# Gate chain with operands in PSUM, whole GpSimd pieces, a later transposition, and a new order of loads and mixes in step 0

## The chip, the core and the metric

One core of one Trainium2 chip. The metric is device microseconds of one launch, as the median of several runs; less is better. The core's engines work side by side, each through its own list of instructions in order: TensorE (PE, matmuls, results in PSUM), VectorE (DVE), ScalarE (ACT), GpSimd (POOL), and SyncE (SP), which here only issues DMAs. [...]

## What is computed

```python
def _attn_ref(x, w_r, w_i, b_r, b_i):              # x: 8 x 2496 x 256
    X = np.fft.rfft(x, axis=1)
    Yr = Xr @ w_r - Xi @ w_i + b_r
    Yi = Xr @ w_i + Xi @ w_r + b_i
    Yr, Yi = (np.sign(v) * np.maximum(np.abs(v) - 0.01, 0) for v in (Yr, Yi))
    return np.fft.irfft(Yr + 1j * Yi, n=2496, axis=1)

def _moe_ref(x, w_gate, w1, w2, capacity):         # x: 19968 x 256, 8 experts, F = 1024
    logits = x @ w_gate
    expert_idx = np.argmax(logits, axis=1)
    gate_w = softmax(logits)[np.arange(N), expert_idx]
    out = np.zeros((N, D))
    for e in range(E):                             # capacity = 80
        tok_idx = the 80 tokens of expert e with the largest gate_w
        out[tok_idx] = gate_w * (relu(x[tok_idx] @ w1[e]) @ w2[e])
    return out
```

A Fourier mix of each of 8 batches, then a mixture of experts of which only 8 x 80 tokens give a row of the output; the other rows are zero.

## The kernel before, in words

The transform of length 2496 = 39 x 64 is done as matmuls. **A** (`stageA`, `stageAz`) does the 39-point part of a batch in 6 calls on loads `xt` (`loadX`, three loads of three DMAs to a batch, two calls of A to each). ACT and DVE split its result into two f16 halves (tile `zs`), which SP stores to the DRAM buffer `zd`. `loadZ` reads `zd` back in another layout (tile `z`). **B** (`stageB`, four calls) does the 64-point part into tile `XT`. **C** (`stageC`, four calls: two halves `eh` of the columns, real and imaginary `ri`) multiplies by the weights, with the soft threshold in the eviction by ACT (`tp`) and DVE (`R`); POOL then makes the sums that `stageTs` forms and tile `YT`. **D** (`stageD`) multiplies by the identity beside the gate's weights, which gives `YO` and the gate's part `Gs`. **HB** (`stageHB`) is the last transform of `YO`, stored to the DRAM tables `hd`.

The gate's logits go through their own small inverse transform, the **gate chain** of a batch: `stageE1a` (sum), `stageE1b` (matmuls, and a trip through DRAM `gd`), `stageE2` (logits, softmax and the choice of the expert, on DVE and ACT) and `stageE3` (a transposition into `sall`). For the last batch `stageG0`, `stageG1` and `stageE1c` replace the first two. `level1` and `level2` pick the largest gates of each expert from `sall`, and the chosen tokens are gathered from `hd` and go through the experts.

A step is one half of a batch's classes: `steps` has 16, (batch, ch). In step i, C of step i stands in the code together with B of step i + 1, D of step i - 1, HB, and A of a later batch (`doC`, `doB`, `doD`, `doHB`, `doA`). A scheduler in the compiler orders each engine's list from that code and its own estimate of times; DMAs given to `pin` keep the order of the code. `psum()` hands out one of four PSUM tiles of 128 x 1024 f32. `zfill` issues the writes of zeros to the output, 56 in all, four in each of steps 1 to 14. `prepW` splits each expert's weights into halves: ACT makes the upper one, POOL (line 788) subtracts it to give the lower one. The output's writes of the chosen rows come last.

The lines that matter: L272 loads of x, L303 stores to `zd`, L314 and L316 loads of `z`, L328 to L330 matmuls of B, L282 of A, L384 of C, L398 C's eviction on DVE, L709 to L719 `stageE2` on DVE, L725 and L728 `stageE3`, L568 and L509 HB, L477 D of the last step, L855 the first instruction of `level1`.

Of the kernel before, what the change touches and what calls it, by code (L numbers as in the profile page):

```python
# [132 lines left out]
def fourier_mix_then_moe(ctx, tc, x, w_r, w_i, b_r, b_i, wg, w1, w2, t1, t2, vq, v3, v0, v1f, vt, sg, cst, cb, out):  # L133
# [133 lines left out]
    def loadX(b, c, xt=None):  # L267
        if xt is None:
            xt = zaq.tile([117, 8, 256], F32, name="xt", bufs=3)
        xv = x[b].rearrange("(a n) d -> a n d", n=64)  # L270
        for s, n in spans(c):
            pin(nc.sync.dma_start(xt[39 * s:39 * s + 39, :n], xv[:, 22 * s + 8 * c:22 * s + 8 * c + n]))  # L272
        return xt
# [11 lines left out]
    zx = []  # L285

    def stageAz(b, q, K, ng, pt):
        if b == 0 and q in (3, 4, 5):
            if q == (3, 4, 5)[0] or (q == 5 and True):
                zx.append(wkb.tile([128, 2, 11, 256], F16, name="YO", bufs=2).rearrange("p h j e -> p (h j e)"))  # L290
            i = (3, 4, 5).index(q) % 2
            zs = zx[-1][:117, 2048 * i:2048 * i + 2048].rearrange("p (g h d) -> p g h d", g=4, h=2)
        else:
            zs = zaq.tile([117, 4, 2, 256], F16, name="zs", bufs=3)
        pv = pt.rearrange("p (g d) -> p g d", d=256)
        nc.scalar.activation(zs[:K, :ng, 0, :], pv[:K, :ng], AF.Copy)  # L296
        nc.vector.tensor_tensor(zs[:K, :ng, 1, :], pv[:K, :ng], zs[:K, :ng, 0, :], op=ALU.subtract)  # L297
        flush()

        def store():  # L300
            for s in range(K // 39):
                n0 = 22 * s + 4 * q
                nc.sync.dma_start(zd[b][:, n0:n0 + ng], zs[39 * s:39 * s + 39, :ng].rearrange("p g h d -> p g (h d)"))  # L303
        stores.append(store)
# [279 lines left out]
    def stageE1a(b, Gs):  # L584
        G = ek.tile([128, 20, 8], F32, name="G", bufs=1)
        nc.vector.tensor_reduce(out=G, in_=Gs.rearrange("p c q (h e) -> p c e (q h)", e=8), op=ALU.add, axis=AX.X)
        gp = ek.tile([128, 2, 20, 8], F16, name="gp", bufs=2)
        nc.scalar.activation(gp[:, 0], G, AF.Copy)
        nc.vector.tensor_tensor(gp[:, 1], G, gp[:, 0], op=ALU.subtract)
        return gp  # L590
# [5 lines left out]
    def stageG0(b, YT):  # L596
# [8 lines left out]
        G = ek.tile([128, 20, 8], F32, name="gex")[:, :11]  # L605
# [6 lines left out]
    def stageG1(b, R, eh):  # L612
# [10 lines left out]
        else:  # L623
            u7 = u7s[0]
            nc.vector.tensor_tensor(u7, pv, u7, op=ALU.add)
# [9 lines left out]
    def stageE1b(b, gp):  # L635
# [7 lines left out]
        gu = ek.tile([128, 2, 48], F32, name="gdif")  # L643
# [4 lines left out]
        nc.scalar.activation(gu, pt[:, 48:144].rearrange("p (t f) -> p t f", t=2), AF.Copy, scale=sc)  # L648
        nc.scalar.activation(gh[:64, 18:21], pt[:64, 512:536].rearrange("p (a e) -> p a e", a=3), AF.Copy, scale=sc)
        nc.vector.scalar_tensor_tensor(gu[:, 1], gu[:, 1], -1.5, at(0), op0=ALU.mult, op1=ALU.add)  # L650
        for a, f in ((1, g), (2, -g)):
            nc.vector.scalar_tensor_tensor(at(a), gu[:, 0], f, gu[:, 1], op0=ALU.mult, op1=ALU.add)
# [42 lines left out]
    def stageE2(b, gr, last=False):  # L695
# [16 lines left out]
        nc.vector.tensor_reduce(out=q, in_=ex, op=ALU.add, axis=AX.X)  # L712
        nc.vector.scalar_tensor_tensor(q, q, 1e-9, unit[:78, 0:1].to_broadcast([78, 32]), op0=ALU.add, op1=ALU.mult)
        nc.vector.reciprocal(q, q)
        rk = rank[:78].unsqueeze(1).to_broadcast([78, 32, 8])
        nc.vector.scalar_tensor_tensor(d, d, 0.0, rk, op0=ALU.is_ge, op1=ALU.mult)
        nc.vector.tensor_reduce(out=m, in_=d, op=ALU.max, axis=AX.X)
        nc.vector.tensor_tensor(d, d, bc(m), op=ALU.is_equal)
        twos.append(nc.vector.tensor_tensor(sc.rearrange("p e n -> p n e"), d, bc(q), op=ALU.mult))  # L719
# [22 lines left out]
    def prepW(e, pool, name):  # L742
# [20 lines left out]
        def step(k, i):  # L763
# [549 lines left out]
    xls.append((Xq[0], loadX(*Xq.pop(0))))  # L1313
# [5 lines left out]
    hold.clear()  # L1319
    preX()  # L1320
# [6 lines left out]
    for i in range(len(steps)):  # L1327
# [26 lines left out]
        def doC(eh, ri, s=None):  # L1354
# [5 lines left out]
            if ri == 1 and b < B - 1:  # L1360
                stageTs(ch, RR[eh], YT, eh)
# [75 lines left out]
        if i == 0:  # L1437
            znext = loadZ(*steps[2])
            hold.clear()
        if i <= 1:  # L1440
            doA(1)
# [4 lines left out]
        if i:  # L1446
            znext = loadZ(*steps[i + 2]) if i + 2 < len(steps) else None
# [46 lines left out]
    stageE3(p[0], sc6)  # L1494
# [6 lines left out]
    with tc.high_priority():  # L1501
        stageE3(b, sc)
# [90 lines left out]
```

## Time and profile before

| | |
|---|---|
| median of 3 runs | 640.14 us (637.53 to 642.4) |
| profiled execution | 635.39 us, of which the span of the instructions is 633.6 us |
| PE busy | 546.1 us, 86% |
| DVE busy | 406.7 us, 64% |
| ACT, POOL busy | 302.7 us, 315.2 us |
| moved by DMA | 133.12 MB, mean 210 GB/s |
| mean granted TensorE clock | 0.931 |

A share of the span is a mean over stages of different kinds: 0 to 100 us the first batches come in, 100 to 500 us the steps run, and then the last gate chain, the choice of tokens and the experts follow each other. So the stages are read one by one.

### The profile page before, as it was taken

The numbers are of one execution on the slowest core, as the hardware profiler recorded it, in microseconds if no ns is written. First come the engines' busy times: TensorE is split into PE (matmuls) and PEld (weight loads), VectorE is DVE, ScalarE is ACT, GpSimd is POOL, SyncE is SP. The second block draws the span as 40 slices with busy tenths as digits, with TensorE's granted clock in tenths as the row PEclk, the third lists the DMA queues.
The fourth block names the chain that finished last, engine by engine and source line by source line (L and its number), as shares of the span: only waits on it lengthen the run. The fifth ranks groups of instructions, "written<-read, shape, count | busy, mean of one in ns | idle before, by whom it ended". The sixth has DMA issues, their size and how long they took to land. (4 is left out here: it accounts for less than half of the span.)

```text
span 633.6 us, 12704 instructions
## 1 busy us (share of the span) xinstructions
PE 546.1 (86%) x4925; PEld 383.8 (61%) x4926; DVE 406.7 (64%) x748; ACT 302.7 (48%) x442; POOL 315.2 (50%) x310
## 2 busy tenths in 40 slices
PE   7366959999999999999999989987899984968791
PEld 2144527676766776686767657765677772526681
DVE  3432525466667667578656996875998847866860
ACT  2322525554545464554446544545566753601560
POOL 2000444444445453544445344575974697647681
PEclk8786978999999999999999999998999975969997
DMA  7796779689679968987997789699754584628830
GB/s 170 268 210 159 205 201 285 196 227 253 200 219 273 267 182 192 304 254 187 249 243 228 199 213 268 169 257 263 238 151 116 150 273 155 204 54 293 297 107 31
DMA packets 95912, 133.12 MB, mean 210 GB/s; under 512 B 26494, under 2 KB 77717, under 8 KB 93973
## 3 DMA queue, kind: packets, MB, share of 16 engines
q1 hardware_dynamic: 88341, 114.59, 67.2%
q10 hardware_dynamic: 5376, 8.39, 4.6%
q0 software_dynamic: 2128, 9.25, 4.3%
q8 instruction: 41, 0.67, 0.4%
q14 instruction: 26, 0.21, 0.1%
HBM read 69.57 MB, written 62.63 MB: 209 GB/s over the span
## 5 line engine op out<-in xcount | busy, mean ns | idle before, releaser
L384 PE MATMUL ps<-XT,WM 128*128 128x288 f16 (+1 forms) x1536 | 217.0, 298 | 8.0 <-DVE R L398 4.7
L384 PEld LDWEIGHTS <-WM 128*128 128x128 f16 x1536 | 149.2, 98 | 66.6 <-issue 12.8
L401 POOL TENSOR_TENSOR R<-R,sgs 128x576 f32<-128x576 f32 x28 | 35.8, 1280 | 183.5 <-DVE R L398 183.4
L398 DVE SCALAR_TENSOR_TENSOR R<-ps,thr,tp 128x674 f32<-128x674 f32 (+1 forms) x56 | 48.4, 864 | 96.1 <-ACT tp L392 94.0
L424 POOL TENSOR_TENSOR YT<-R,YT 128x1408 f16<-128x1408 f32 (+1 forms) x28 | 73.5, 2624 | 36.3 <-ACT YT L423 36.3
L392 ACT ACTIVATE tp<-ps,thr 128x674 f32<-128x674 f32 (+1 forms) x64 | 49.7, 777 | 87.5 <-PE ps L384 87.2
L282 PE MATMUL ps<-xt,t1f 117*117 117x512 f32 (+1 forms) x170 | 86.2, 634 | 3.9 <-DMA xt<-in_x 3.9
L328 PE MATMUL ps<-t2s,z 128*128 128x128 f16 (+1 forms) x320 | 60.3, 225 | 28.8 <-DMA z<-zd 21.1
L297 DVE TENSOR_TENSOR zs<-ps,zs 117x1024 f16<-117x1024 f32 (+1 forms) x45 | 51.0, 1135 | 27.2 <-ACT zs L296 26.1
L334 DVE TENSOR_TENSOR XT<-ps,XT 128x640 f16<-128x640 f32 (+2 forms) x64 | 51.9, 814 | 15.1 <-ACT XT L333 15.1
L296 ACT ACTIVATE zs<-ps 117x1024 f16<-117x1024 f32 (+1 forms) x45 | 43.0, 957 | 38.8 <-PE ps L282 34.7
L333 ACT ACTIVATE XT<-ps 128x640 f16<-128x640 f32 (+2 forms) x64 | 44.9, 702 | 33.9 <-PE ps L330 22.7
L329 PE MATMUL ps<-t2s,z 128*128 128x128 f16 (+1 forms) x320 | 60.2, 225 | 0.0
L330 PE MATMUL ps<-t2s,z 128*128 128x128 f16 (+1 forms) x320 | 60.1, 225 | 0.0
L328 PEld LDWEIGHTS <-z 128*128 128x128 f16 (+1 forms) x320 | 32.1, 100 | 37.5 <-DMA z<-zd 21.2
L423 ACT ACTIVATE YT<-R 128x1408 f16<-128x1408 f32 (+1 forms) x28 | 35.5, 1268 | 36.2 <-POOL R L420 35.9
L534 PE MATMUL ps<-YO,vqs 128*128 128x512 f16 (+1 forms) x252 | 49.5, 338 | 3.3 <-DVE R L398 3.3
L492 DVE TENSOR_TENSOR YO<-ps,YO 128x768 f16<-128x768 f32 (+1 forms) x50 | 45.3, 906 | 5.2 <-ACT YO L491 5.2
L282 PEld LDWEIGHTS ps<-xt,t1f 117*117 117x117 f32 (+1 forms) x170 | 29.2, 188 | 31.4 <-issue 30.3
L481 PE MATMUL ps<-wgi,YT 128*128 128x136 f16 (+1 forms) x302 | 42.8, 225 | 1.0 <-POOL YT L424 1.0
L534 PEld LDWEIGHTS <-vqs 128*128 128x128 f16 x252 | 24.9, 101 | 30.6 <-issue 14.4
L480 PE MATMUL ps<-wgi,YT 128*128 128x144 f16 (+1 forms) x302 | 43.2, 229 | 0.0
(274 smaller groups left out, 939.9 us busy)
## 6 DMA issues: line engine op xcount, KB each, us to landing
out<-zero SPq DMA_DIRECT2D x48, 384.0 KB
hd<-hs SPq DMA_DIRECT2D x94, 192.0 KB
zd<-zs SPq DMA_DIRECT2D x114, 156.0 KB
xt<-in_x SPq DMA_DIRECT2D x48, 312.0 KB
z<-zd SPq DMA_DIRECT2D x16, 576.0 KB
wt<-in_moe_w ACTq DMA_DIRECT2D x10, 512.0 KB
z<-zd SPq DMA_DIRECT2D x7, 704.0 KB
z<-zd SPq DMA_DIRECT2D x7, 640.0 KB
```

The costliest lines, as they stand in the source:

```text
L282: nc.tensor.matmul(pt[:K, 512 * j:512 * j + 512], t1f[:K, :K], xv[:, 2 * j:2 * j + 2], start=True, stop=True)
L297: nc.vector.tensor_tensor(zs[:K, :ng, 1, :], pv[:K, :ng], zs[:K, :ng, 0, :], op=ALU.subtract)
L328: nc.tensor.matmul(o, zz(0), t2s[:K, cl, 0, :], start=True, stop=False)
L329: nc.tensor.matmul(o, zz(0), t2s[:K, cl, 1, :], start=False, stop=False)
L330: nc.tensor.matmul(o, zz(1), t2s[:K, cl, 0, :], start=False, stop=True)
L334: nc.vector.tensor_tensor(ov(1), pv, ov(0), op=ALU.subtract)
L384: nc.tensor.matmul(pt[:, 512 * k:512 * k + n], WM[:, dh, m, wh, 128 * eh:128 * eh + 128], XT[:, dh, xh, c, c0 + n * k:c0 + n * k + n], sta ...
L392: nc.scalar.activation(fv(t), pv, AF.Relu, bias=thr[:, eh, ri, 0:1])
L398: nc.vector.scalar_tensor_tensor(fv(Rf), pv, thr[:, eh, ri, 1:2], fv(t), op0=ALU.add, op1=ALU.min)
L424: nc.gpsimd.tensor_tensor(yv(1), rv, yv(0), op=ALU.subtract)
L492: dvs.append(nc.vector.tensor_tensor(yol, yy, yoh, op=ALU.subtract))
L534: nc.tensor.matmul(o, tab[:, v], yo(h), start=(i == 0), stop=(i == 2))
```

## The change

Three groups of edits. In step 0 and ahead of it: the first load of x is cut in two along the order in which A uses it; all three loads of batch 1 are issued before step 0, those of batch 2 only after `loadZ` of batch 1 (list `hold`); step 0 is written out on its own, with A of batch 1 between its C, then B of step 1, `loadZ`, and the last C; step 1 gets two more A; the writes of zeros start in step 3, and steps 3 to 10 have five each. In the gate chain: the intermediate tiles that DVE reads and writes lie in PSUM (`G`, `u7`, `best`, `place`, `qs`), `stageE1b` reads PSUM without the copy to `gu`, and `stageE2` finds the expert before it needs the exponentials. And `prepW` gives POOL whole pieces of 1024 columns instead of four of 256 for experts 2 to 7, and `stageE3` of batch 6 stands behind D and HB of the last step, next to that of batch 7.

```diff
@@ loadX
-        for s, n in spans(c):
-            pin(nc.sync.dma_start(xt[39 * s:39 * s + 39, :n], xv[:, 22 * s + 8 * c:22 * s + 8 * c + n]))
+        cuts = (0, 4, 8) if (b, c) == (0, 0) else (0, 8)
+        for lo, hi in zip(cuts, cuts[1:]):
+            for s, n in spans(c):
+                pin(nc.sync.dma_start(xt[39 * s:39 * s + 39, lo:min(hi, n)], xv[:, 22 * s + 8 * c + lo:22 * s + 8 * c + min(hi, n)]))
@@ stageE1a
-        G = ek.tile([128, 20, 8], F32, name="G", bufs=1)
+        G = psum()[:, :160].rearrange("p (c e) -> p c e", e=8)
@@ stageG0
-        G = ek.tile([128, 20, 8], F32, name="gex")[:, :11]
+        G = pt[:, 512:600].rearrange("p (c e) -> p c e", e=8)
@@ stageG1
-            u7 = u7s[0]
-            nc.vector.tensor_tensor(u7, pv, u7, op=ALU.add)
+            u7 = pt[:, 512:632].rearrange("p (t f) -> p t f", t=5)
+            nc.vector.tensor_tensor(u7, pv, u7s[0], op=ALU.add)
@@ stageE1b
-        nc.scalar.activation(gu, pt[:, 48:144].rearrange("p (t f) -> p t f", t=2), AF.Copy, scale=sc)
...
-        nc.vector.scalar_tensor_tensor(gu[:, 1], gu[:, 1], -1.5, at(0), op0=ALU.mult, op1=ALU.add)
+        nc.vector.scalar_tensor_tensor(gu, pt[:, 96:144], -1.5 * sc, at(0), op0=ALU.mult, op1=ALU.add)
         for a, f in ((1, g), (2, -g)):
-            nc.vector.scalar_tensor_tensor(at(a), gu[:, 0], f, gu[:, 1], op0=ALU.mult, op1=ALU.add)
+            nc.vector.scalar_tensor_tensor(at(a), pt[:, 48:96], f * sc, gu, op0=ALU.mult, op1=ALU.add)
@@ stageE2
-        nc.vector.tensor_reduce(out=q, in_=ex, op=ALU.add, axis=AX.X)
-        nc.vector.scalar_tensor_tensor(q, q, 1e-9, unit[:78, 0:1].to_broadcast([78, 32]), op0=ALU.add, op1=ALU.mult)
+        best, place, = (pt[:78, 256 * k:256 * k + 256].rearrange("p (n e) -> p n e", e=8) for k in (1, 2))
+        qs = pt[:78, 768:800]
+        rk = rank[:78].unsqueeze(1).to_broadcast([78, 32, 8])
+        nc.vector.tensor_tensor(best, L, bc(m), op=ALU.is_ge)
+        nc.vector.tensor_tensor(place, best, rk, op=ALU.mult)
+        nc.vector.tensor_reduce(out=m, in_=place, op=ALU.max, axis=AX.X)
+        nc.vector.tensor_tensor(best, place, bc(m), op=ALU.is_equal)
+        nc.vector.tensor_reduce(out=qs, in_=ex, op=ALU.add, axis=AX.X)
+        nc.vector.tensor_scalar(q, qs, 1e-9, None, op0=ALU.add)
         nc.vector.reciprocal(q, q)
-        rk = rank[:78].unsqueeze(1).to_broadcast([78, 32, 8])
-        nc.vector.scalar_tensor_tensor(d, d, 0.0, rk, op0=ALU.is_ge, op1=ALU.mult)
-        nc.vector.tensor_reduce(out=m, in_=d, op=ALU.max, axis=AX.X)
-        nc.vector.tensor_tensor(d, d, bc(m), op=ALU.is_equal)
-        twos.append(nc.vector.tensor_tensor(sc.rearrange("p e n -> p n e"), d, bc(q), op=ALU.mult))
+        twos.append(nc.vector.tensor_tensor(sc.rearrange("p e n -> p n e"), best, bc(q), op=ALU.mult))
@@ prepW
-                m = 256 if e >= 2 else 1024
-                for j in range(0, 1024, m):
-                    nc.gpsimd.tensor_tensor(wl[:, k, c + j:c + j + m], wt[:, j:j + m], wh[:, k, c + j:c + j + m], op=ALU.subtract)
+                nc.gpsimd.tensor_tensor(wl[:, k, c:c + 1024], wt, wh[:, k, c:c + 1024], op=ALU.subtract)
@@ ahead of the steps
-    xls.append((Xq[0], loadX(*Xq.pop(0))))
+    for _ in range(2):
+        xls.append((Xq[0], loadX(*Xq.pop(0))))
...
     znext = loadZ(*steps[1])
-    hold.clear()
-    preX()
+    xls.append((Xq[0], loadX(*Xq.pop(0))))
+    hold.append(1)
@@ step 0, instead of the mix of the other steps
+            doC(0, 0); doA(2)
             consts2()
+            doC(0, 1, None, False); doA(2)
+            doC(1, 0); doA(2)
+            flush()
+            with tc.issue_after(evs[-1].ins):
+                stageTs(ch, RR[0], YT, 0)
+            for _ in Bl:
+                doB()
+            znext = loadZ(*steps[2])
+            hold.clear()
+            preX()
+            doC(1, 1)
+            prev = (b, ch, YT)
+            XT = XTn
+            continue
@@ the first of the four places of zfill() in a step; the other three have the first edit alone
-        if i > 0:
+        if i > 2:
+            zfill()
+        if 3 <= i <= 10:
             zfill()
@@ behind the steps
-    stageE3(p[0], sc6)
     doHB()
...
     with tc.high_priority():
+        stageE3(p[0], sc6)
         stageE3(b, sc)
```

**SP, step 0, what stands ahead of the load of `z` for batch 1.** `zd_85` is batch 1's buffer, `xt` a load of x, `z_650` and `z_602` the tile of step 2. Before, behind the first three stores of batch 1:

```order
L272 DMA xt<-in_x 39x1536 x2
L272 DMA xt<-in_x 39x1024
L303 DMA zd_85<-zs 39x2048 x6
L272 DMA xt<-in_x 39x2048 x3
L303 DMA zd_85<-zs 39x2048 x6
L272 DMA xt<-in_x 39x2048 x3
L303 DMA zd_85<-zs 39x1024 x2
L314 DMA z_650<-zd_85 64x11x512
```

and now, from the last constant on:

```order
L237 DMA cbs<-in_cb 128x10
L306 DMA zd_85<-zs 39x2048 x12
L306 DMA zd_85<-zs 39x1024 x2
L317 DMA z_602<-zd_85 64x11x512
L319 DMA z_602<-zd_85 64x10x512
L274 DMA xt<-in_x 39x2048 x6
L317 DMA z_994<-zd_85 64x9x512
```

The two loads of batch 2 (the rows 39x2048 x3) stood ahead of the load of `z` and stand behind it now; no load of x lies between batch 1's stores any more.

**DVE, step 0.** Each row ends one piece of PE's work, and PE's list has the pieces in nearly the same order: `XT` is B, `zs` is A, `R` is C. Before, from the end of step 0's own B on:

```order
L334 TENSOR_TENSOR XT<-ps,XT 128x2x320 x2
L398 SCALAR_TENSOR_TENSOR R<-ps,thr,tp_132 128x674
L334 TENSOR_TENSOR XT<-ps,XT 128x2x320
L297 TENSOR_TENSOR zs<-ps,zs 117x4x256
L334 TENSOR_TENSOR XT<-ps,XT 128x2x320
L398 SCALAR_TENSOR_TENSOR R<-ps,thr,tp_133 128x674
```

and now:

```order
L300 TENSOR_TENSOR zs<-ps,zs 117x4x256 x2
L401 SCALAR_TENSOR_TENSOR R<-ps,thr,tp_132 128x674
L401 SCALAR_TENSOR_TENSOR R<-ps,thr,tp_133 128x674
L300 TENSOR_TENSOR zs<-ps,zs 117x4x256 x2
L401 SCALAR_TENSOR_TENSOR R<-ps,thr,tp_132 128x674
L300 TENSOR_TENSOR zs<-ps,zs 117x4x256
L300 TENSOR_TENSOR zs<-ps,zs 78x2x256
L337 TENSOR_TENSOR XT<-ps,XT 128x2x320 x2
L337 TENSOR_TENSOR XT<-ps,XT 128x2x256 x2
L401 SCALAR_TENSOR_TENSOR R<-ps,thr,tp_133 128x674
L401 SCALAR_TENSOR_TENSOR R<-ps,thr,tp_132 128x576
```

All six A of batch 1 stand ahead of the first B of step 1, which was the second piece; the last row, step 1's first C, stands ahead of step 2's B.

**PE, the last gate chain.** `hs` is the last batch's transformed gate, the rows with `gr` and `Gs` behind it are `stageE3` of batches 7 and 6. Before:

```order
L699 MATMUL ps<-hs_6211,v1fs 78x256
L699 MATMUL ps<-hs_6211,v1h 78x256
L725 MATMUL ps<-ident,Gs 128x78 x2
L568 MATMUL ps<-YO,v3s 128x512
L568 MATMUL ps<-YO,v3s 128x256
L477 MATMUL ps<-ident,R 128x128 x18
```

and now, where the 24 rows of L512 that follow here are not shown:

```order
L701 MATMUL ps<-hs_6189,v1fs 78x256
L701 MATMUL ps<-hs_6189,v1h 78x256
L571 MATMUL ps<-YO,v3s 128x512
L571 MATMUL ps<-YO,v3s 128x256
L480 MATMUL ps<-ident,R 128x128 x18
```

```order
L731 MATMUL ps<-ident,Gs 128x78 x2
L731 MATMUL ps<-ident,gr 128x78 x2
L571 MATMUL ps<-YO,v3s 128x512
L571 MATMUL ps<-YO,v3s 128x256
```

HB and D follow the last batch's logits at once; both transpositions, of batch 6 and of batch 7, stand behind them.

## Rows read from the trace of the kernel before

**Rows 1.** Stages: busy us of each engine, granted clock, DMA share, GB/s.

```profile
44.50:52.30 7.80, 0.00 (x0) 0.00 (x1) 0.92 (x1) 0.82 (x1) 0.00 (x0) 0.70 1.00 186
...
52.33:57.82 5.49, 5.49 (x24) 3.18 (x25) 0.82 (x1) 0.90 (x2) 0.00 (x0) 0.50 0.75 182
...
92.59:98.78 6.19, 6.19 (x17) 2.61 (x18) 0.86 (x1) 1.02 (x1) 0.00 (x0) 0.50 0.95 227
...
126.00:153.00 27.00, 27.00 (x223) 18.74 (x222) 16.33 (x22) 13.58 (x17) 11.66 (x10) 1.00 0.95 248
```

**Rows 2.** PE in steps 0 and 1, in order of time; in brackets idle time and what ended it.

```profile
52.33 0.27 PE L328 MATMUL ps<-t2s,z 128*128 128x128 f16 x1 [7.87 <-DMA z<-zd]
...
58.38 0.22 PE L330 MATMUL ps<-t2s,z 128*128 128x128 f16 x1
58.43 3.64 PE L384 MATMUL ps<-XT,WM 128*128 128x337 f16 x24
...
78.69 3.66 PE L282 MATMUL ps<-xt,t1f 117*117 117x512 f32 x8 [0.50 <-DMA xt<-in_x]
...
92.59 0.29 PE L328 MATMUL ps<-t2s,z 64*128 64x128 f16 x1 [7.29 <-DMA zd<-zs]
```

**Rows 3.** SP's issues of DMAs, 28 to 101 us, in order of time.

```profile
30.97 1.40 SPq L272 DMA_DIRECT2D xt<-in_x  x3
...
79.58 0.72 SPq L303 DMA_DIRECT2D zd<-zs  x2
86.09 0.59 SPq L314 DMA_DIRECT2D z<-zd  x1
```

**Rows 4.** The page's DMA issues: count and size of one.

```profile
out<-zero SPq DMA_DIRECT2D x48, 384.0 KB
...
xt<-in_x SPq DMA_DIRECT2D x48, 312.0 KB
```

**Rows 5.** DVE, two rows of the last step, then the last gate chain, in order.

```profile
505.43 0.76 DVE L407 TENSOR_TENSOR R<-tp,XT 128x576 f32<-128x576 f32 x1 [1.45 <-ACT XT L403]
...
506.29 1.04 DVE L409 TENSOR_TENSOR R<-R,sgs 128x576 f32<-128x576 f32 x1
...
519.77 0.41 DVE L710 TENSOR_TENSOR gdif<-ps,gm 78x256 f32<-78x256 f32 x1
...
524.42 6.38 DVE L716 SCALAR_TENSOR_TENSOR gdif<-gdif,rank 78x256 f32<-78x256 f32 x1
...
534.13 0.41 DVE L716 SCALAR_TENSOR_TENSOR gdif<-gdif,rank 78x256 f32<-78x256 f32 x1
...
541.54 0.87 DVE L855 MAX8 cv<-sall 128x8 f32<-128x312 f32 x2
```

**Rows 6.** POOL's subtractions by shape: busy us, mean ns of one.

```profile
L788 POOL TENSOR_TENSOR pair<-wt,pair 128x1024 bf16<-128x1024 f32 x8 | 17.2, 2144 | 5.0 <-ACT pair L780 5.0
L788 POOL TENSOR_TENSOR pair<-wt,pair 128x256 bf16<-128x256 f32 x20 | 13.1, 683 | 0.0
```

**Rows 7.** POOL at the end of the steps, first and last of seven such rows.

```profile
504.21 3.65 POOL L788 TENSOR_TENSOR pair<-pair,pair 128x256 bf16<-128x256 f32 x4 [4.07 <-ACT pair L780]
...
525.46 5.04 POOL L788 TENSOR_TENSOR pair<-pair,pair 128x256 bf16<-128x256 f32 x8
```

**Rows 8.** PE in the last gate chain, in order of time.

```profile
522.64 1.05 PE L699 MATMUL ps<-hs,v1h 39*78 39x256 f32 x2
532.85 0.52 PE L725 MATMUL ps<-ident,Gs 78*128 78x78 f32 x2 [9.16 <-DVE Gs L719]
533.17 2.85 PE L568 MATMUL ps<-YO,v3s 128*128 128x512 f32 x4
...
540.80 0.35 PE L725 MATMUL ps<-ident,gr 78*128 78x78 f32 x2
```

**Rows 9.** DVE's groups of instructions, 120 to 500 us: busy us, mean ns of one, idle before.

```profile
L719 DVE TENSOR_TENSOR gr<-gdif,gq 78x256 f32<-78x256 f32 x6 | 14.5, 2411 | 0.2
```

**Rows 10.** The longest of PE's waits, 120 to 500 us: us in total, times, longest.

```profile
PE ps L384 <- DVE R L398: 4.7, 3, 2.4
```

More of the change, by code (lines that the diff above doesn't have):

```diff
@@ L285, in fourier_mix_then_moe @@
     zx = []
+    evs = []
     def stageAz(b, q, K, ng, pt):
@@ L295, in stageAz @@
         pv = pt.rearrange("p (g d) -> p g d", d=256)
-        nc.scalar.activation(zs[:K, :ng, 0, :], pv[:K, :ng], AF.Copy)
+        evs.append(nc.scalar.activation(zs[:K, :ng, 0, :], pv[:K, :ng], AF.Copy))
         nc.vector.tensor_tensor(zs[:K, :ng, 1, :], pv[:K, :ng], zs[:K, :ng, 0, :], op=ALU.subtract)
@@ L642, in stageE1b @@
         gh = ek.tile([128, 21, 8], F32, name="gh", bufs=1)
-        gu = ek.tile([128, 2, 48], F32, name="gdif")
+        gu = ek.tile([128, 48], F32, name="gdif")
         sc = 2.0 / S / XS
@@ L1352, in fourier_mix_then_moe, with doC @@
         RR = {}
-        def doC(eh, ri, s=None):
+        def doC(eh, ri, s=None, sums=True):
             if ri == 0:
@@ L1360, in doC @@
             if ri == 1 and b < B - 1:
-                stageTs(ch, RR[eh], YT, eh)
+                if sums:
+                    stageTs(ch, RR[eh], YT, eh)
             elif ri == 1 and not end:
@@ L1406, in fourier_mix_then_moe @@
         pend = [(p[0], stageE1b(*p)) for p in pend]
-        if i > 0:
+        if i > 2:
             zfill()
         doC(0, 1); doD(); doHB(); doB(); doD()
-        if i == 0:
-            doA(3)
         doP(); doW({12: 1, 13: 1, 14: 1}.get(i, 1))
-        if i > 0:
+        if i > 2:
             zfill()
@@ L1419, in fourier_mix_then_moe @@
         sc = None
-        if i > 0:
+        if i > 2:
             zfill()
-        if i == 0:
-            doA(1)
         doC(1, 1)
-        if i == 0:
-            hold.append(1)
         doA(); doHB()
-        if i == 0:
-            flush()
         if pend and not end:
@@ L1436, in fourier_mix_then_moe @@
             pend3 = [(p[0], sc)]
[L1437 to L1441, printed above, removed]
+        if i == 1:
+            doA(2)
         if prev and pch == 1:
@@ L1445, in fourier_mix_then_moe @@
             doHB()
-        if i:
-            znext = loadZ(*steps[i + 2]) if i + 2 < len(steps) else None
+        znext = loadZ(*steps[i + 2]) if i + 2 < len(steps) else None
         if p1 is None and not (Aq or Xq or xls):
```

## Prediction

> **What bounds the kernel now.** The page comes first: PE is busy for 86% of 633.6 us, so about 88 us are PE's waits and its lower clock, and the question is where they lie. The table of stages and PE's list in time put the first ones ahead of 100 us. PE stands still for 7.87 us ahead of 52.33 and for 7.29 us ahead of 92.59, each time until a tile `z` is there [rows 2]. In the first of these stretches PE did nothing while the DMA engines' share was 1.00 at 186 GB/s [rows 1]: data, not PE, set the pace. [...] With the 0.50 us for a load of x [rows 2] the two places cost 7.87 + 7.29 + 0.50 of idle time and half of 5.49 and of 6.19 in slow work: 21.5 us in all.
>
> The list of SP's DMAs tells why `z` is late. For the first it stands behind a load of x of batch 1, issued at 30.97; for the second it was issued at 86.09, 6.5 us after the last stores of `zd` at 79.58 that it needs; PE could start another 6.5 us later, at 92.59 [rows 2, 3]. The stores came late because A of batch 1 was spread over step 0, its last calls at 78.69 [rows 2].
>
> From 100 to 500 us PE works without a gap to speak of: 27.00 of 27 us in the stretch from 126 us, with the DMA engines at 0.95 of their time there [rows 1]. An edit there pays only through PE's waits, of which the longest group is 4.7 us in 380 [rows 10].
>
> The second place is the last gate chain. PE has the last batch's logits at 523.69 (522.64 + 1.05) and then waits 9.16 us, for `Gs` [rows 8]. DVE's list shows what it does meanwhile: one instruction, L716 of batch 6, takes 6.38 us, and the same instruction of batch 7 at 534.13 takes 0.41 [rows 5]. POOL subtracts weights without a gap from 504.21 to 530.50 (525.46 + 5.04) [rows 7], and L716 ends 0.3 us after that. It has two inputs in SBUF; L710, with one input in PSUM, took 0.41 in the midst of POOL's work [rows 5]. So I read it as DVE locked out by POOL. Behind the wait come `stageE3` of batch 6, HB and D of the last step, and only at 540.80 `stageE3` of batch 7 [rows 8]; `level1` starts at 541.54 [rows 5]. From there to the end runs one chain of DVE, DMA and experts, which the change shifts but for POOL's weights.
>
> [...]
>
> **The change, part by part.**
>
> *Step 0.* All six A of batch 1 now stand ahead of the first B of step 1. The first load of x of batch 1 is issued where it was, at about 31 us; with 312 KB each [rows 4], three DMAs take 5.0 us at 186 GB/s, and the second three stand behind them. I let A start at 42.5 and put the rest by PE's prices. Six A at 1.83 (half of 3.66) less the short last one, 10 us; two C of step 0 that are left and stand among them, 7.3; that gives the last A at about 63 with some 3 us for loads. B of step 1 has 54 matmuls, 0.055 us apart (58.38 to 58.43), 3 us; C(1,1) and step 1's first C 3.64 each [rows 2]: PE comes to the B of step 2 at 72.8. The last stores are issued a little over a us after A's end and need the 6.5 us of before to land (79.58 to 86.09 [rows 3]), so they are there at 71 to 73; the load of `z` then takes the 6.5 us of before, and B can start at 77 to 81. I take 79.5. PE is idle for 6.7, has half of some 6.2 us at the lower clock (3.1), and finds the load of batch 2's x, now behind `z`, about 2.8 late (0.94 MB at 227 GB/s [rows 1], 4.1 us, with little of B to do meanwhile). With 0.4 for small waits that is 13.0 against 21.5: **−8.5**. If `z` comes at 76 and the clock stays up, about 8 are left of the 21.5 (−13); if it comes at 87, 14.2 + 3.1 + 2.8 + 0.4 (−1).
>
> *The first load cut in two* saves at most what A's first call waits for, while its third still needs the whole; SP issues three more DMAs. 0, ±1, in the range.
>
> *Zero writes.* Steps 1 and 2 lose eight, steps 3 to 10 gain one each, 384 KB [rows 4], 1.55 us of all DMA engines at 248 GB/s. The stretch of 27 us at 0.95 and 248 GB/s [rows 1] has 1.35 us free; the mean of the span is 210 GB/s, so others have more. **+1**, from 0 (hidden) to +4 (0.2 us too much in some steps, and `z` late).
>
> *Gate chain of batches 0 to 5.* L719 takes 2.41 us there [rows 9] against 0.41 of L710 [rows 5]; it now has a PSUM operand. The chain loses some 2 us of DVE per batch, and PE waited for DVE's `R` 4.7 us in all [rows 10]. One more DVE instruction per chain costs 0.4, and the PSUM slot is held for some 4 us, with three others free. **−2**, from 0 to −4.
>
> *Whole pieces on POOL.* A piece of 1024 takes 2.14 us, one of 256 takes 0.68 [rows 6]: POOL's sum falls (four are 2.7), but an instruction of DVE with two SBUF inputs that meets one may wait up to 2.14. In the last step L409 at 506.29 took 1.04 where L407 ahead of it, of the same size, took 0.76 [rows 5], on the path to the last gate. Three or four such instructions stand there: **+1.5**, 0 to +5. `level1` has them too: **+1**, 0 to +3. The experts' last pieces end later: **+0.5**, 0 to +1.5.
>
> [...]
>
> *The last gate chain.* L716 and its followers get an operand in PSUM, so the price is that of L710, 0.41, and the chain of batch 7, whose rows stood behind those of batch 6, can begin at 523.7. Ten instructions of about 0.4 with one trip to ACT end it at about 529. PE in the meantime does HB and D, which took 7.6 us from 533.17 to 540.80 [rows 8]: from 523.7 to 531.3. Now PE is what ends last; both `stageE3` follow at once (0.52 + 0.35), then one copy more than the 0.4 us between 541.15 and `level1`, which starts at 533.3 in place of 541.54: **−8**. If POOL still holds half of L716's wait the chain ends at 532 and −7 is left; if whole pieces stop DVE's few instructions left with two SBUF operands, −4; at best, if HB and D go quicker with no wait ahead of them, −11.
>
> [...]
>
> **The sum.** −8.5 + 1 − 2 + 1.5 + 1 + 0.5 − 8 = −14.5. The profiled execution took 635.4 us, so it would take 620.9; the median stands 4.7 above it, and I put the same difference on it: 640.1 − 14.5 = **625.6**.
>
> **Rivals.** *The start stays bound by the DMA engines* (0.14): the same bytes pass before `z`, at a share of 1.00 [rows 1]; what moves is their order, and two loads of x come earlier. Then `z` of step 2 is not there before 87, the first part is −1 to −3, and with the rest −6: about 632. For it: the first wait had nothing but DMA in it; against: the second is put down to a store's landing [rows 2], and that store moves. *The best case* (0.12): `z` at 76 and full clock, −13, and −10 in the tail: 616. *Whole pieces lock DVE out* (0.08): each of some ten instructions with two SBUF inputs in the last step and `level1` waits 1.5 us longer (2.14 − 0.68 [rows 6]), +15 in place of the +2.5 above: 640.1 − 14.5 + 12.5, about 638. It decides once such waits fall on the path at every meeting. *PSUM operands don't free DVE* (0.02): the edit doesn't do what it says, L716's wait remains, and `stageE3` moved back can't help; middle and tail bring nothing: 640.1 − 8.5 + 1 = 633. *The denser zero writes* (0.05), the slower side: once the DMA engines' share in a step of 28 us passes 1 (1.55 us more at 0.95 is 1.007), the load of `z` falls behind from step to step; a wait of 1.6 us may then be followed by some 5 us lost in slow work besides (5.49 and 6.19 us at 0.50 cost 3 each [rows 1], twice that at the most). In four steps that is 26 us: 651. Against it: the next stretches have more room, and the loads of `z` are issued a step ahead.
>
> **How the numbers follow.** The forecast has 0.59. Its own terms reach from 613 (−13, −10, −4) to 632; the rivals at 632 and 633 lie inside a range of **613 to 637**, which leaves out the slower side (0.05), most of the rival at 638 (0.08) and some 0.05 of spread between runs (637.5 to 642.4 before). About 1% is what a measurement of this kernel can tell from no change: faster means below 633.7. Forecast and best case are (0.71), and of the two near 632 and 633 (0.16) somewhat over half, 0.09: faster 0.80; the rest of them and the rival at 638 make same 0.15; slower 0.05.
>
> **What would show it.** Right: the first B of step 2 starts near 79.5, with one long wait of PE ahead of it, and the wait at 52 is gone; L716's successors take about 0.4 while POOL works; PE goes from the last logits into HB without a gap, and the first row of `level1` starts some 16 us earlier than 541.5 (8.5 from the start, 8 from the tail, less the middle). Wrong: `z` of step 2 past 85; DVE instructions of 2 us and more at 505 to 515 or in `level1`; waits of PE for `z` in steps 3 to 10; POOL's work lasting longer into the gate chain.

## The result, and the profile after

The changed kernel took 635.75 us (median of 20 runs, 629.3 to 640.64), the kernel before 640.85 (20 runs): ratio 0.9899, 95% interval 0.9873 to 0.9924, or 6.5 us less (4.9 to 8.1) where 14.5 were forecast. The ratio leaves out runs in a slower state, so it is not that of the medians, and the profiled execution of the changed kernel is such a run: 640.64 us with a span of 638.9, the longest of its 20. Each reading of it below is therefore set beside the profiles of the experiments; of those, e3's is 4 us above the median of its runs and e8's 6 us below.

The start. PE's list in time, as in [rows 2]: start, us, line, operation, and in brackets idle time and what ended it.

```profile
47.54 1.95 PE L284 MATMUL ps<-xt,t1f 117*117 117x512 f32 x4 [3.03 <-DMA xt<-in_x]
...
83.82 0.23 PE L331 MATMUL ps<-t2s,z 64*128 64x128 f16 x1
...
85.47 0.23 PE L331 MATMUL ps<-t2s,z 128*128 128x128 f16 x1 [1.31 <-DMA z<-zd]
...
92.93 3.73 PE L284 MATMUL ps<-xt,t1f 117*117 117x512 f32 x4 [6.45 <-DMA xt<-in_x]
```

The wait of 7.87 us is gone; 3.03 us for x stand in its place, ahead of the first A of batch 1. B of step 2, which started at 92.59, starts at 83.82 and has the rest of its `z` at 85.47. But the A between the first two B of step 2 waits for x until 92.93, which is where PE stood before, and its four matmuls then take 3.73 us at a granted clock of 0.50 (eight took 3.66 in the kernel before [rows 2], where the clock was 1.00 from 78.69 to 82.35). The two stretches by stage, as in [rows 1], with the granted clock as a share of TensorE's full speed, and SP's issues ahead of them, as in [rows 3]:

```profile
80.79:93.00 12.21, 4.45 (x45) 3.35 (x42) 2.69 (x3) 3.67 (x4) 7.06 (x5) 0.75 1.10 176
92.93:97.00 4.07, 4.07 (x7) 1.30 (x7) 0.00 (x0) 0.30 (x1) 0.00 (x0) 0.50 0.80 160
```

```profile
65.00 8.67 SPq L306 DMA_DIRECT2D zd<-zs  x14
75.80 0.58 SPq L317 DMA_DIRECT2D z<-zd  x1
76.44 0.64 SPq L319 DMA_DIRECT2D z<-zd  x1
77.12 2.94 SPq L274 DMA_DIRECT2D xt<-in_x  x6
```

Six DMAs of x, two loads, follow `z` at once; the DMA engines' share is 1.10, at 176 GB/s, over the 12.21 us that end with PE's wait.

The tail. PE and DVE in the last gate chain, as in [rows 8] and [rows 5]; DVE's tiles named `ps` lie in PSUM, the others in SBUF:

```profile
534.01 0.94 PE L701 MATMUL ps<-hs,v1h 39*78 39x256 f32 x2
534.88 2.86 PE L571 MATMUL ps<-YO,v3s 128*128 128x512 f32 x4
...
541.79 0.35 PE L731 MATMUL ps<-ident,Gs 78*128 78x78 f32 x2
```

```profile
515.88 1.52 DVE L410 TENSOR_TENSOR R<-tp,XT 128x576 f32<-128x576 f32 x1 [1.45 <-ACT XT L406]
...
518.07 1.93 DVE L412 TENSOR_TENSOR R<-R,sgs 128x576 f32<-128x576 f32 x1
...
536.75 0.42 DVE L719 TENSOR_TENSOR ps<-ps,rank 78x256 f32<-78x256 f32 x1
...
542.76 0.87 DVE L858 MAX8 cv<-sall 128x8 f32<-128x312 f32 x2
...
544.00 1.77 DVE L867 TENSOR_TENSOR V<-mod,cv 128x256 f32<-128x256 f32 x1
...
546.16 1.88 DVE L867 TENSOR_TENSOR V<-mod,cv 128x256 f32<-128x256 f32 x1
547.97 2.09 DVE L826 CAST tk<-ci 128x16 f32<-128x16 uint32 x1
550.09 2.05 DVE L824 SCALAR_TENSOR_TENSOR tk<-tk,unit 128x16 f32<-128x16 f32 x1
552.17 0.17 DVE L830 SCALAR_TENSOR_TENSOR tk<-tk,tk 128x16 f32<-128x16 f32 x1
```

The wait of 9.16 us [rows 8] is gone: PE passes from the last logits (534.95) into HB, and the chain's instructions take 0.18 to 0.62 (L719 0.42) while POOL works. `level1` begins 7.8 us after the last logits, where it was 17.8. Then four of its instructions take 1.77 to 2.09, one after another, until POOL's last piece ends. POOL's list:

```profile
545.46 2.30 POOL L791 TENSOR_TENSOR pair<-wt,pair 128x1024 bf16<-128x1024 f32 x1
547.73 4.38 POOL L791 TENSOR_TENSOR pair<-pair,pair 128x1024 bf16<-128x1024 f32 x2
```

In the steps between, DVE's group of [rows 9] is down from 2411 to 600 ns:

```profile
L725 DVE TENSOR_TENSOR gr<-ps,gq 78x256 f32<-78x256 f32 x6 | 3.6, 600 | 0.2
```

### The profile page after: what moved, and what is told of

It is laid out like the page before. It is cut to its first block, busy times and chain, and to the rows that moved or that the text cites. A ratio compares the mean times of both kernels' runs of the same rounds, so it can differ in the third digit from the quotient of the medians.

```text
span 638.9 us, 12640 instructions
## 1 busy us (share of the span) xinstructions
PE 551.1 (86%) x4926; PEld 385.4 (60%) x4926; DVE 395.5 (62%) x756; ACT 300.1 (47%) x435; POOL 301.3 (47%) x250
## 5 line engine op out<-in xcount | busy, mean ns | idle before, releaser
L387 PE MATMUL ps<-XT,WM 128*128 128x288 f16 (+1 forms) x1536 | 223.3, 303 | 11.0 <-ACT hs L542 5.1
L387 PEld LDWEIGHTS <-WM 128*128 128x128 f16 x1536 | 151.7, 100 | 72.5 <-issue 15.8
L404 POOL TENSOR_TENSOR R<-R,sgs 128x576 f32<-128x576 f32 x28 | 35.8, 1278 | 180.6 <-DVE R L401 142.4
L284 PEld LDWEIGHTS ps<-xt,t1f 117*117 117x117 f32 (+1 forms) x170 | 28.9, 188 | 42.8 <-issue 42.3
```

Source lines behind the costliest of these rows:

```text
L284: nc.tensor.matmul(pt[:K, 512 * j:512 * j + 512], t1f[:K, :K], xv[:, 2 * j:2 * j + 2], start=True, stop=True)
L387: nc.tensor.matmul(pt[:, 512 * k:512 * k + n], WM[:, dh, m, wh, 128 * eh:128 * eh + 128], XT[:, dh, xh, c, c0 + n * k:c0 + n * k + n], sta ...
```

## The experiments

Each kernel ran beside the kernel before on the same chip. This table has the ratio with its interval and, from the one profiled execution of each, the length in us of seven stretches: to the first C of step 2; steps 2 to 10; steps 11 to 14; the last step to its last logits; from there to the first row of `level1`; to the first of the flattening matmuls that end the choice of tokens; to the end.

| | ratio | to step 2 | 2–10 | 11–14 | last step | to `level1` | to flattening | to the end |
|---|---|---|---|---|---|---|---|---|
| before | 1 | 119.7 | 260.5 | 109.0 | 34.5 | 17.8 | 18.4 | 73.6 |
| changed | 0.990 (0.987–0.992) | 120.6 | 262.0 | 115.8 | 36.6 | 7.8 | 23.0 | 73.1 |
| e1 first load whole | 0.991 (0.988–0.994) | 118.2 | 262.7 | 113.9 | 37.1 | 8.2 | 23.0 | 71.7 |
| e2 pieces of 256 | 0.998 (0.995–1.002) | 117.8 | 260.6 | 113.6 | 33.4 | 8.8 | 26.9 | 72.9 |
| e3 fills as before | 0.985 (0.981–0.989) | 117.5 | 257.2 | 114.5 | 39.7 | 7.8 | 22.8 | 72.5 |
| e4 tail alone | 0.993 (0.991–0.996) | 120.3 | 262.8 | 106.4 | 35.8 | 7.8 | 25.4 | 73.7 |
| e5 POOL only writes | 0.966 (0.963–0.970) | 120.5 | 260.7 | 114.0 | 28.9 | 6.9 | 16.1 | 76.9 |
| e6 `level1` in PSUM | 0.976 (0.971–0.980) | 120.2 | 255.6 | 110.0 | 36.0 | 8.1 | 19.6 | 78.5 |
| e7 start alone | 0.998 (0.995–1.001) | 119.1 | 258.5 | 118.4 | 35.1 | 12.8 | 19.5 | 77.9 |
| e8 later A | 0.973 (0.970–0.977) | 110.2 | 255.6 | 109.3 | 36.6 | 8.1 | 23.0 | 75.2 |
| e9 e6 and e8 | 0.961 (0.957–0.966) | 113.6 | 255.6 | 112.9 | 35.9 | 8.3 | 16.2 | 73.6 |
| e10 one A more | 0.987 (0.983–0.991) | 113.4 | 266.0 | 109.3 | 37.8 | 8.6 | 16.5 | 79.7 |
| e11 no late fills | 0.983 (0.979–0.986) | 114.3 | 262.5 | 113.6 | 38.8 | 8.3 | 16.2 | 74.7 |
| e12 transposition | 0.996 (0.992–1.000) | 120.2 | 261.1 | 113.9 | 35.8 | 12.4 | 18.8 | 74.4 |

A stretch differs by some 2 us between profiles without a reason in the code (the first one by where the loads of x fall), steps 11 to 14 and the last step by up to 4 (109.3 in e8 and 112.9 in e9; 39.7 in e3 and 36.6 in e8), so single differences under that mean nothing.

### The parts of the change, one by one

**e1.** `cuts = (0, 8)` in `loadX`.

> The changed kernel with the first load of x whole again. Theory (the cut lets PE start early, then leaves it idle until the third call's x, and the lower clock that follows costs about 3 us): A of batch 0 ends near 21.2 and no longer at 25.2 us, the first B at 32.5, and 3 to 4 us of that stay to the end: ratio to before about 0.984 (the change itself 0.990). Rival (PE waits for later loads anyway): A ends earlier, but the first B of step 2 and the A behind it still start at 85 and 93 us: ratio 0.990.

The rival held: A of batch 0 ended at 21.45 and not at 25.23, the first B of step 2 came at 78.5, and A behind it still waited for x, to 89.6. The cut does cost there. PE in e3, which has it:

```profile
6.39 1.95 PE L284 MATMUL ps<-xt,t1f 117*117 117x512 f32 x4 [0.80 <-DMA xt<-in_x]
8.75 1.95 PE L284 MATMUL ps<-xt,t1f 117*117 117x512 f32 x4 [0.41 <-DMA xt<-in_x]
15.19 5.33 PE L284 MATMUL ps<-xt,t1f 117*117 117x512 f32 x8 [4.50 <-DMA xt<-in_x]
```

Two calls run early, PE then stands for 4.5 us until the third call's x is there at 15.19 (14.95 in the kernel before), and the eight matmuls behind that take 5.33 us, where the second eight took 3.66 in the kernel before. The end of the kernel doesn't see it.

**e2.** The loop over pieces of 256 in `prepW` again.

> The changed kernel with POOL's subtractions in pieces of 256 again. Theory (whole pieces lock DVE out for a whole piece): the four instructions of level1 that took 1.8 to 2.1 us fall to 1 or less, L412 of the last step from 1.93 to about 1: 4 to 6 us less than the change, ratio to before about 0.983. Rival (POOL needs longer in small pieces, 2.7 for 2.14, and its backlog moves with it): the waits are shorter and more, ratio 0.988 to 0.993.

Both were wrong, the other way: 0.998, 5.4 us slower than the change. The profile shows 3.9 us of it between `level1` and the flattening (26.9 for 23.0). DVE and then POOL in `level1`:

```profile
535.53 10.71 DVE L869 TENSOR_TENSOR V<-mod,cv 128x256 f32<-128x256 f32 x1
...
546.63 0.40 DVE L869 TENSOR_TENSOR V<-mod,cv 128x256 f32<-128x256 f32 x1
546.96 0.16 DVE L828 CAST tk<-ci 128x16 f32<-128x16 uint32 x1
```

```profile
533.37 5.07 POOL L793 TENSOR_TENSOR pair<-pair,pair 128x256 bf16<-128x256 f32 x8
538.41 2.54 POOL L793 TENSOR_TENSOR pair<-wt,pair 128x256 bf16<-128x256 f32 x4
540.91 5.05 POOL L793 TENSOR_TENSOR pair<-pair,pair 128x256 bf16<-128x256 f32 x8
```

One instruction waited 10.3 of its 10.71 us, to the end of POOL's run at 545.96, through some 16 pieces; the same instruction took 0.40 as soon as POOL was done. That is L716 of [rows 5] in another place. In the tail of the changed kernel, with whole pieces of 2.1 to 2.3 us, DVE got in behind each: its four instructions above took 1.77 to 2.09.

Small pieces did so too, at other places. First the same instruction in the kernel before, where POOL subtracts pieces of 256 without a gap from 534.79 to 548.25; then, from e7, where POOL does so from 529.38 to 553.76, L719, which is L716 of [rows 5], and again the instruction of `level1`:

```profile
542.79 0.93 DVE L864 TENSOR_TENSOR V<-mod,cv 128x256 f32<-128x256 f32 x1
...
544.11 0.42 DVE L864 TENSOR_TENSOR V<-mod,cv 128x256 f32<-128x256 f32 x1
```

```profile
532.56 0.91 DVE L719 SCALAR_TENSOR_TENSOR gdif<-gdif,rank 78x256 f32<-78x256 f32 x1
...
545.15 0.91 DVE L867 TENSOR_TENSOR V<-mod,cv 128x256 f32<-128x256 f32 x1
```

Each lost some 0.5 us at most, less than one piece (0.67 us in the kernel before, twelve in 8.03). So a run of small pieces shut DVE out to its end twice, for 6.38 us (some nine pieces of 683 ns [rows 6]) and for 10.71 us (some 16), but it didn't at every meeting, and what decides between the two isn't shown.

**e3.** `zfill` as before, four in each of steps 1 to 14.

> The changed kernel with the writes of zeros four in each of steps 1 to 14 again. Theory (the extra write in steps 3 to 10 makes the trips of the gate through DRAM late, PE's waits for gr that are 8 us in the changed kernel's trace against 0.6): these waits fall to below 2 us, and with 1 to 2 us more for z in steps 1 and 2 the ratio is 0.980 to 0.985. Rival (those waits differ from run to run, or come from the gate chain's own edits): they stay, and the ratio is 0.990 to 0.995.

0.985 to 0.990: 3.1 us, with intervals that overlap a little (0.9809 to 0.989 and 0.9873 to 0.9924). Steps 2 to 10 are where it shows: 260.6 to 262.7 us in the five profiles with the extra writes and the new start (the changed kernel, e1, e2, e5, e12), 255.6 to 258.5 in the five without them (e3, e6 to e9). The waits for `gr` fell from 8.1 to 2.2 us of PE. The writes are not all of it: the kernel before and e4, with four writes a step and the old start, take 260.5 and 262.8 us for the same steps, and e4 waits 3.2 us for `gr` there.

**e4.** The gate chain, POOL's pieces and the transposition of the change; loads, step 0 and writes of zeros of the kernel before.

> The kernel before with the gate chain in PSUM, the whole pieces and the later transposition, and with loads, step 0 and writes of zeros as before. Theory (the tail gained 10.0 us up to level1 and gave 2.1 in the last step and 4.6 in level1 back, the start nothing): ratio 0.992 to 0.996. Rival 1 (the start is what gained, and the tail nothing): 1.000. Rival 2 (the PSUM slots that the gate chain now holds stop PE in the steps): waits of PE behind ACT's evictions of 5 us and a ratio over 1.000.

0.993, as the theory had it: 10.0 us won to `level1`, 7.0 given back behind it.

**e7.** The converse: loads and step 0 of the change in the kernel before.

> The kernel before with the new loads and step 0 alone; writes of zeros, gate chain and POOL as before. Theory (the start is bound by the DMA engines: PE's idle time up to step 2 is 34 us before and after, in other places): the first B of step 2 starts at 78 to 80 in place of 92.6, but A behind it waits for x until 90, and 0 to 2 us are left: ratio 0.997 to 1.000. Rival (the forecast's step: 8.5 us less): 0.987.

0.998, 1.4 us (3.3 less to 0.4 more). PE's waits in that start:

```profile
46.50 3.73 PE L284 MATMUL ps<-xt,t1f 117*117 117x512 f32 x4 [4.32 <-DMA xt<-in_x]
...
73.33 6.58 PE L387 MATMUL ps<-XT,WM 128*128 128x337 f16 x48 [1.16 <-DVE XT L337]
...
81.07 0.23 PE L331 MATMUL ps<-t2s,z 64*128 64x128 f16 x1 [1.16 <-DMA z<-zd]
84.36 0.29 PE L331 MATMUL ps<-t2s,z 128*128 128x128 f16 x1 [2.95 <-DMA z<-zd]
90.44 3.73 PE L284 MATMUL ps<-xt,t1f 117*117 117x512 f32 x4 [4.30 <-DMA xt<-in_x]
```

Summed over PE's list, PE is idle for 33.95 us ahead of the second half of step 1's C, 33.97 in the kernel before. The first C of step 2 comes at 119.1 us for 119.7, with two matmuls of A, 0.9 us, still to be done that the kernel before has done by then. The 12.8 us to `level1`, for 17.8 with the same code in the tail, go with L719's 0.91 us above: where L716 was shut out for 6.38 us and PE waited 9.16 for `Gs` [rows 8], PE waits 4.91 here.

**e12.** `stageE3(p[0], sc6)` ahead of `doHB()` again.

> The changed kernel with the transposition of batch 6 ahead of HB and D of the last step again. Theory (DVE is no longer locked out in the gate chain, so the order of PE now decides: batch 6's gates are ready 3.8 us after the last logits, and PE would wait that long with HB and D behind it): a wait of PE of 2 to 4 us comes back ahead of the transposition, the first row of level1 starts that much later against the last logits (7.8 us in the changed kernel, 10 to 12 here), ratio 0.992 to 0.996 in place of 0.990. Rival (level1 waits for POOL in any case, so a later start costs nothing): the first row of level1 is later and the flattening matmuls are not, ratio 0.990.

PE waits 4.24 us for `Gs`, and `level1` starts 12.4 us after the last logits instead of 7.8, but behind it 18.8 us follow instead of 23.0, since more of POOL's work is over. Logits to flattening are 31.3 and 30.8 us, which is the rival; the ratio, 0.996, lies on the theory's side. The profile and the times don't decide it.

### What holds the two places

**e5.** `nc.gpsimd.memset(wl[:, k, c:c + 1024], 0.0)`, issued behind ACT's upper half, in place of the subtraction.

> The changed kernel in which POOL, in place of each subtraction of 1024 columns, writes zeros to the lower half of the weights behind ACT's upper half; the lower halves are left out of the result, and POOL reads nothing. Theory (DVE's instructions with two SBUF inputs wait for a POOL instruction that reads SBUF): the rows of level1 that took 1.8 to 2.1 us fall to 0.2 to 0.5, from the first row of level1 to the flattening matmuls it is 17 us and not 23, ratio to before 0.978 to 0.983 (the change: 0.990). Rival 1 (POOL's writes stop DVE too): these rows last as long as one of POOL's writes. Rival 2 (that stretch is bound by something else than DVE): the rows get short and the time stays at 0.990.

More than expected: 0.966. From `level1` to the flattening 16.1 us, and the last step, which neither side had named, 28.9 for 36.6. A write took 0.95 us, so POOL's work was also over ahead of `level1`; that DVE isn't stopped by writes is seen at two places only. L446 and L447 took 0.56 and 0.55 us beside four writes from 490.25 to 493.88 (L444 and L445, of the same size, took 2.37 and 2.38 beside subtractions in the changed kernel), and in the last step L410 began at 509.83 beside two writes that ran from 508.60 to 510.44:

```profile
509.83 0.76 DVE L410 TENSOR_TENSOR R<-tp,XT 128x576 f32<-128x576 f32 x1 [1.45 <-ACT XT L406]
...
510.70 0.75 DVE L412 TENSOR_TENSOR R<-R,sgs 128x576 f32<-128x576 f32 x1
```

These two took 1.52 and 1.93 beside subtractions in the changed kernel.

**e6.** In `level1(1)`, writes of zeros as before:

```diff
+            tp_ = psum()
+            nc.scalar.activation(tp_[:, 0:32], mod32, AF.Copy)
...
-                nc.vector.tensor_tensor(cm[:, h], mod32.unsqueeze(2)...
+                nc.vector.tensor_tensor(cm[:, h], tp_[:, 0:32].unsqueeze(2)...
...
+            f, fb, q, ne = (P[:, 64 + 16 * v:80 + 16 * v]... for v in range(4))
```

> The changed kernel with the writes of zeros as before (0.985 to before) and, in addition, the second operands of level1 (the mask, two constants and four of the seven small tiles) in PSUM, copied there by ACT. Theory (the lock took back in level1 what it gave in the gate chain): the rows of level1 take 0.2 to 0.4 us while POOL works, the stretch from level1 to the flattening matmuls is 16 to 18 us in place of 22.8, ratio 0.975 to 0.979. Rival (what follows waits for the positions' stores and loads in any case): 0.983 to 0.986.

0.976, by the theory. With POOL at work to 538.9:

```profile
534.25 0.76 DVE L877 TENSOR_TENSOR V<-ps,cv 128x256 f32<-128x256 f32 x2 [2.61 <-ACT ps L862]
535.04 0.18 DVE L831 CAST ps<-ci 128x16 f32<-128x16 uint32 x1
```

The rows are short; 2.61 us went to the wait for ACT's copy, so the stretch is 19.6 and not 16.

**e8.** In step 1, writes of zeros as before:

```diff
-        doC(0, 0); doB(); doA(); doHB(); doB()
+        doC(0, 0); doB(); doHB(); doB()
...
         doC(0, 1); doD(); doHB(); doB(); doD()
+        doA()
```

> The changed kernel with the writes of zeros as before (0.985 to before) and the first A of step 1 behind its second C, B and D instead of between the two B. Theory (PE stands for 5 us ahead of that A, with C and B behind it ready): the wait for x falls under 1 us, the second C of step 1 starts 4 us earlier, and 2 to 4 us stay: ratio 0.979 to 0.982. Rival (the DMA engines set the pace of the whole start, so the wait comes back at the next load of z or x): idle time up to 120 us stays at 34 us, ratio 0.985.

0.973, 7.6 us less than e3 and better than the theory: C and B run while x comes in, and the longest wait there is 3.14 us (4.96 in e3), with the granted clock at 1.00 (0.88). 42 to 92 us in e8, then 42 to 100 us in e3, by stage:

```profile
42.00:92.00 50.00, 39.95 (x299) 25.83 (x297) 18.85 (x21) 18.76 (x24) 16.62 (x13) 1.00 0.88 206
```

```profile
42.00:100.00 58.00, 43.66 (x297) 27.18 (x295) 19.58 (x22) 19.45 (x24) 14.47 (x11) 0.88 0.90 202
```

Nearly the same work (299 and 297 matmuls), 50 and 58 us, at a clock of 1.00 and 0.88; the DMA engines are as busy in both (0.88 and 0.90), and A's x is there no earlier to speak of (A starts at 89.02 and at 90.01). The gain stands in other profiles too: to the first C of step 2 it is 110.2 to 114.3 us in e8 to e11, which have the later A, and 117.5 to 120.6 in all that have the new start without it.

**e9.** e6 and e8 together, the two copies to PSUM by DVE (0.20 and 0.15 us).

> The later A of step 1 and the operands of level1 in PSUM together (copied there by DVE), writes of zeros as before. Theory (two places far apart, one at the start and one in the tail): the gains add. Behind a ratio of 0.985, the later A brought 0.012 and level1 0.009, of which a wait of 2.6 us for ACT's copy goes as well: 0.960 to 0.965. Rival (level1's wait was as long as it was because POOL's work lay there, and an earlier tail meets more of POOL): 0.968 to 0.973.

0.961 (618.03 us median): they add, and `level1` to flattening is 16.2, as with no POOL work beside it in e5. This is the fastest kernel of the study, 18 us under the changed one.

**e10 and e11.** Two tries, both on the kernel of e9, at the wait of 4 to 6 us for ACT's evictions of HB in step 12, which the other profiles with the new step 0 and the gate chain in PSUM have and e4 has not (0.4): `doA(3)` for `doA(2)` in step 1; and writes of zeros five in each of steps 1 to 11 and one in step 12.

> The kernel of the run before with three A and not two at the end of step 1, so that all A are done as early in the steps as in the kernel before and the loads of the experts' weights start half a step earlier. Theory (in every run with the new step 0, PE waits 4 to 6 us for ACT's evictions of HB in step 12, since the weights' loads start some 8 us later there and meet the stores that free those tiles): that wait falls under 1 us, ratio 4 us lower than that of the run before, 0.954 to 0.958. Rival (another cause): the wait stays, the ratio is the same within 0.003.

> The same kernel as e9 with the writes of zeros five in each of steps 1 to 11 and one in step 12, so none in steps 13 and 14. Theory of the extra write (a fifth write in a step costs PE some 0.5 us a step, as in the changed kernel): steps 3 to 10 get longer by about 4 us, ratio 0.966 to 0.970. Rival (the wait for ACT's evictions of HB in step 12 comes from the writes of zeros that stand ahead of those stores): that wait goes, 4 to 5 us are won and 4 lost: 0.960 to 0.963.

With the third A the wait went from 4.2 to 0.5 us, as expected of its cause; but a wait of 5.6 us for DVE's `R` came up in the same steps. The early A stands ahead of its x (two waits of 2 us, at 110 and 120), and steps 2 to 10 took 10 us more than in e9, of which the second of these waits and 4.3 us for `gr` are some 6: 0.987, not 0.954. With no late writes the wait stayed (6.6), so they aren't its cause, and the fifth write cost steps 2 to 10 6.9 us: 0.983, slower even than the theory.

## Why the prediction was wrong

The direction was right and 635.75 lies in the range; the size was less than half of the forecast. Of its signs, the wait at 52 us went, `z` of step 2 came in time and PE went from the last logits into HB without a gap; but `level1` began at 542.76, not 16 us before 541.5, and DVE instructions of 2 us came in `level1`. By its terms:

**Step 0, −8.5: this is the step that failed; −1.4 (e7).** The first B of step 2 came at 78 to 82 in the profiles with the new step 0 (at 84 in the changed kernel's own and in e9), as the step had it (79.5), but by two errors that cancel. The last A of batch 1 ended at 67.2 in the changed kernel and not at 63; and SP issued the load of `z` 2.1 us after the last store (65.00 + 8.67 to 75.80), where the step kept the 6.5 us of before (5.8 counted the same way).

What fell was "finds the load of batch 2's x ... about 2.8 late". I charged three DMAs, 0.94 MB, at 227 GB/s. Six stood behind `z`, 1.87 MB, of which A needs the first three, and from 85.47 to 92.93, while A waited, the engines moved 156 GB/s. So A waited until 90 to 93, 4.3 us in e7 and 6.5 in the changed kernel, in e7 on top of 1.2 and 3.0 us for the two parts of `z`; the four matmuls behind it took 3.73 us in both, at a clock of 0.50 in the changed kernel. The sum also left out the 3 us for loads that the same paragraph puts ahead of the last A; in e7 PE waited 4.32 us there, at 46.50. From 40 to 98 us PE is idle for 16.0 us in the kernel before and 13.9 in e7, where the step has 9.9 (6.7 + 2.8 + 0.4); e8, with one A further back, has 10.05. The half that the step charges at a clock of 0.50 agrees with A's matmuls: four took 3.73 us at 0.50, eight 3.66 at 1.00 [rows 2].

The first rival (the start stays bound by the DMA engines) had the size right (−1 to −3), and its mechanism wrong: `z` came well before 87, and e8 moves the same bytes at the same rate (206 GB/s for 202 in e3) and wins 7.6 us, since what held PE was one A that stood in its list ahead of work that was ready.

**Writes of zeros, +1: right in sign, mis-sized; +3.1 (e3), 4 to 5 in steps 2 to 10.** They fell on the gate's trips through DRAM (waits for `gr` of 8.1 us, 2.2 in e3) rather than on `z`; e4, which waits for `gr` without them, leaves open how much of that is theirs.

**Gate chain of batches 0 to 5, −2: not decided.** Its instruction got shorter (2411 to 600 ns). But with the new start, e7, without the new chain, needs 258.5 us for steps 2 to 10, and e3, e6, e8 and e9, with it, 255.6 to 257.2; with the old start it is the other way, 260.5 before and 262.8 in e4. PE's longest wait for `R` there, 2.4 us before, is 2.2 in e3.

**Whole pieces, +3 in all: wrong in sign; −5.4 (e2).** I priced a meeting with small pieces at 0.68 us at the most and with whole ones at 2.14, one piece each: my estimate from [rows 6]. Both held where DVE got in behind a piece (waits of 0.5 us, and of up to 1.9). What they leave out is that a run of small pieces shut DVE out to its end, for 10.3 us in e2: the row of 6.38 us [rows 5], about nine pieces of 683 ns [rows 6], stood in the prediction and got no price. For the last step alone the price of +1.5 was about right or small: 35.8 to 39.7 us with whole pieces, 33.4 to 35.1 with small ones (before, e2, e7).

**The last gate chain, −8: right against the profile of the kernel before, −10.0 to `level1`, and in part luck. `level1`, +1: mis-sized; +4.6.** Against e7, whose old chain wasn't shut out, the gain to `level1` is 5.0 (12.8 to 7.8); and e12, with the new chain and the old order of PE, has 12.4. So the operands in PSUM took away the long wait where it occurred (6.38 us before, 0.42 for each of L718 and L719, which replace L716, in the changed kernel), and in the profiles without one it is the later transposition that gained. `level1` now starts 8 us deeper in POOL's work, which didn't move. This is where half of the tail's gain went (4.6 of 10.0, 7.0 in e4), and e6 and e9 show that the lock took it: the stretch is 16.2 us in e9, with the operands in PSUM, and 23.0 in e8.

**Left open.** Steps 11 to 14 take 109 to 118 us with the new step 0, 106 to 109 without; the forecast had nothing there, and in the profiles of the changed kernel and of e7 they are 6.8 and 9.4 us longer than before. So e7's −1.4 holds a loss there besides; but up to the first C of step 2 it had gained only 0.6. 1.8 us are A matmuls that stand later. Of the waits, e10 ties one to how early A ends; its steps took 109.3 us, as in e8, which has that wait. The parts measured alone (−1.4, −4.4, +3.1) sum to −2.7, the whole is −6.5; intervals of 2 us on each cover most of that. When a run of small pieces shuts DVE out, and when it lets it in, is open too.

## What to carry to other kernels

When a list is bound by loads, look for the first instruction in it that waits for data with ready work behind it: moving that one (e8, 7.6 us) was worth more here than reordering all the loads (e7, 1.4 us). Taking the wait of 6.38 us in front of the lock away moved the waiting to the next instructions that met it, four of 1.77 to 2.09 us in `level1`; follow the chain up to where the other engine's work ends, and free all of it (e6 and e9: 19.6 and 16.2 us for 23.0). And cutting POOL's work into small pieces didn't make it yield at every meeting (0.5 us lost at some, 6.0 and 10.3 at others): read from several traces whether the other engine gets in between them.

## What the runs showed that was not expected

- POOL's instructions of 0.63 us back to back shut out one DVE instruction with two SBUF inputs for 10.3 us, while the same instruction lost 0.5 us beside such a run in two other profiles; with instructions of 2.1 to 2.3 us, in the changed kernel, DVE got in after each of them.
- A load cut so that PE can start 3 us earlier made A of the first batch end 1 to 4 us later: behind the idle time that it opened, eight matmuls took 5.33 to 6.75 us instead of 3.66.
- POOL's subtractions, put in place of writes, cost 15.5 us in the last step and the choice of tokens: 67.4 us from the last step to the flattening in the changed kernel, 51.9 in e5, where each of POOL's instructions is also shorter (0.95 us for 2.1). The operands of `level1` in PSUM gave back about half (60.4 in e9).
